# A two-layer spectral and gated-MLP kernel: forward stage in written order with its loads pinned, filter loads without marker copies, row sums from PSUM

## The chip, the cores and the metric

The kernel runs on one core of one Trainium2 chip. The metric is the device time of one execution in microseconds (us). The kernel before took 1263.59 us in the median of three runs (1261.65 to 1268.51). Engines are called by short names: PE is the matmul engine (PEld its weight load), DVE the vector engine, ACT the scalar engine, POOL the GpSimd engine; SP only issues DMAs. SBUF is the on-chip memory, PSUM the eight accumulator banks that PE writes.

## The reference

The input x has 2048 rows of 512 float32 numbers. Two layers follow each other, with the same weights; a layer is a spectral filter and then a bilinear gated MLP, each with a layer norm ahead and a residual sum behind:

```
def _A_ref(x, w_r, w_i):
    X = rfft2(x);  X = X * (w_r + 1j * w_i)
    return irfft2(X, s=(S, D))
def _B_ref(x, w_gate, w_up, w_down):
    return ((x @ w_gate) * (x @ w_up)) @ w_down
x = x + _A_ref(_layernorm(x), A_w_r, A_w_i)
x = x + _B_ref(_layernorm(x), B_w_gate, B_w_up, B_w_down)
...
```

The last two lines are done twice. S is 2048, D is 512, and the MLP is 1792 wide.

## The kernel before, in words

The residual `xs` stays in SBUF as 16 tiles of 128 rows by 512. Each layer goes through these stages:

**Forward stage** (`fwd_steps`, lines 211 to 282). For each tile t: `stats` (bn_stats and bn_aggr on DVE), `rstd` (a square root on ACT and four small DVE instructions), `a0` (loads the twiddle factors `tw`; the half sums and differences `fo`, `fe` of the row on POOL and DVE), `a1` (four transposes `tp` on PE, copied to `fs` by ACT), `a2` (eight instructions of the row transform `dp` on PE, scaled to `us` by ACT), `a3` (eight instructions of the first column transform `sp` on PE into two PSUM banks, copied into `E` by ACT). The work is listed as steps: a tile's `a0`, `a1`, `a2` and `a3` belong to steps b, b+1, b+2 and b+4, and the list is sorted by step. Lines 671 to 683 issue it for the first layer and put between its entries the loads of the spectral filter (`W.load`, 1 MB each, lines 290 to 302) and the splitting of the first two MLP weight blocks (`forms_w`, lines 509 to 533: `rg` is the block as loaded, `wt` its high and low parts; ACT copies the high part, POOL subtracts). A filter load is preceded by a marker, a copy of one element of `E` by POOL into the load's target, so that the load cannot be issued before that tile of `E` is there; `prep_hp` (lines 144 to 151) has a marker too. The twiddle tiles and the small table `wct` share four buffers (tag `tw`).

**Middle phase** (`mid_phase`): the second column transform, the product with the filter, and the way back, over 16 groups of columns. It begins with DVE transposes of `E`, which need all 16 tiles.

**Inverse stage** (`inv_steps`): back to rows (`vp`, `vs`, `yi`), the sum into `xs`, and the next statistics.

**MLP** (`unit`, `beside`, `down_w`): for each of 14 weight blocks seven products (`gx`, `gy`, `gw`, `gz`, `gv`; a Strassen-like scheme, with three float32r matmuls each) and the down product `db`, added to `xs` by DVE. `db` has two PSUM banks (tag `d`), so that the third `db` in a row waits for DVE's sum of the first. Rows are done in two halves. While the first half runs, the rows of the second are normalised (`norm`, which writes `xn`), transposed by PE (`turn`, which writes `tq` into banks of tag `a`, three of them), copied by ACT into `xf` (`stage["t"]`, line 450) and summed (`sums`, lines 471 to 476: four DVE instructions of 128 by 256, all operands in SBUF). `weave` (lines 654 to 665) mixes two lists by the costs that stand in them; the row-sum entry is listed at 0.3.

What sets the order: a scheduler may move instructions on each engine, unless they were issued while `pin["on"]` was set (lines 111 to 130), when they keep the written order among themselves. The MLP runs pinned (line 717). The first forward stage, the end of the second one (lines 766 and 767), the middle phases and the first part of each inverse stage run unpinned. DMA issues on SP are never pinned. Every engine's queue is in order once it is built. All recorded operations carry line 123, that of the helper; the tiles' names tell them apart.

Of the kernel before, what the change touches and what calls it, by code (L numbers as in the profile page):

```python
# [9 lines left out]
F32 = mybir.dt.float32  # L10
F32R = mybir.dt.float32r
AF = mybir.ActivationFunctionType
ALU = mybir.AluOpType
EPS = 1e-5
NF = 14
G0 = [(0,), (1,), (2,), (3,)] + [(t, t + 1) for t in range(4, 16, 2)]
# [71 lines left out]
def kernel(ctx: ExitStack, tc: tile.TileContext, x, wf, wc, wb, dfwd, dinv, tf, ti, mid, out):  # L88
    nc = tc.nc
    PS = bass.MemoryType.PSUM  # L90
    cp = ctx.enter_context(tc.tile_pool(name="cp", bufs=1))
    wk = ctx.enter_context(tc.tile_pool(name="wk", bufs=1))
# [3 lines left out]
    XYW = "xyw"  # L96

    def bank(name, tag):
        return pp.tile([128, 512], F32, name=name, tag=tag, bufs=NB[tag])
# [4 lines left out]
    def f32(ap):  # L104
        return ap.bitcast(F32)
# [2 lines left out]
        for n, (a, b) in enumerate(((sh, mh), (sh, ml), (sl, mh))):  # L108
            TE.matmul(o, a, b, start=start and n == 0, stop=stop and n == 2, skip_group_check=True)

    pin = {"on": False}

    class Queue:


        def __init__(self, engine):
            self.engine = engine

        def __getattr__(self, name):
            f = getattr(self.engine, name)  # L120

            def call(*args, **kw):
                ins = f(*args, **kw)  # L123
                if pin["on"]:
                    tc.keep_in_program_order(ins)
                return ins

            return call

    V, A, G, TE = (Queue(e) for e in (nc.vector, nc.scalar, nc.gpsimd, nc.tensor))  # L130
    tt, stt = V.tensor_tensor, V.scalar_tensor_tensor
    gtt = G.tensor_tensor

# [7 lines left out]
    f2, g2, ident = (midt[:, 128 * i:128 * i + 128] for i in range(3))  # L141
    hp = cp.tile([128, 2, 32, 2], F32, name="hp")

    def prep_hp(after):
        wct = wk.tile([128, 4, 2, 32], F32, name="wct", tag="tw", bufs=4)
        G.tensor_copy(wct[0:1, 0, 0, 0:1], after)
        nc.sync.dma_start(wct, wc)
        for ri, col, src, op, scale in ((0, 0, 0, ALU.add, 0.5), (1, 0, 1, ALU.subtract, 0.5),
                                        (0, 1, 3, ALU.subtract, -0.5), (1, 1, 2, ALU.add, 0.5)):
            tt(hp[:, ri, :, col], wct[:, src, 0], wct[:, src, 1], op)  # L150
            V.tensor_scalar(hp[:, ri, :, col], hp[:, ri, :, col], scale, None, op0=ALU.mult)
# [49 lines left out]

    def twiddle(src, t):
        tw = wk.tile([128, 2, 128], F32, name="tw", tag="tw", bufs=4)
        nc.sync.dma_start(tw, src[:, 2 * t:2 * t + 2])
        return tw

    def in_steps(ops):
# [76 lines left out]
    class Filter:  # L284
# [2 lines left out]
        def __init__(self):  # L287
            self.at = {}

        def load(self, n, after=None):  # L290
            if n < 3:
                if n == 0:
                    self.a = wk.tile([128, 3, 64, 32], F32, name="wq", tag="xA")
                self.at[n] = self.a[:, n]
            elif n < 6:
                t = wk.tile([128, 64, 32], F32, name="wr", tag=("dc", "h", "wd")[n - 3])
                self.at[n] = t
            else:
                self.at[n] = self.a[:, n - 6]
            if after is not None:  # L300
                G.tensor_copy(self.at[n][0:1, 0, 0:1], after)
            nc.sync.dma_start(self.at[n], wf[:, n // 2, n % 2])

        def __call__(self, n, i, lo=0):
            kw = 16 * (n % 4)
# [127 lines left out]
    def build_x(X, nm, tags, stage=None):  # L433

        XA, XS = X
        s = {}
        r = nm["ts"][0] % 4
        cols = slice(128 * r, 128 * r + 128)

        def norm():  # L440
            s["xn"] = [normed(t, nm) for t in nm["ts"]]

        def turn(h):
            tq = bank("tq", tags[h])
            xn = s["xn"][h]
            for i in range(4):
                TE.transpose(tq[:, 128 * i:128 * i + 128], xn[:, 128 * i:128 * i + 128], ident)
            s[h] = tq.rearrange("p (b k s) -> p b k s", b=2, k=2)
            if stage is not None:
                A.copy(stage["t"][:, r, 2 - 2 * h:4 - 2 * h], s[h])  # L450

        def forms():
            a, b = s[0], s[1]
            S = wk.tile([128, 4, 2, 128], F32, name="sx", tag=("sx", "rg")[r % 2])
            A.copy(S[:, 1:4:2], a)
            A.copy(S[:, 2], b[:, 0])
            A.copy(S[:, 0], b[:, 1])
            A.copy(XA[:, 1:3, 0, :, cols], a)
            A.copy(XA[:, 0, 0, :, cols], b[:, 1])
            gtt(S[:, 0], S[:, 2], S[:, 0], ALU.add)  # L460
            gtt(S[:, 2], S[:, 1], S[:, 2], ALU.subtract)
            gtt(S[:, 1], S[:, 0], S[:, 1], ALU.subtract)
            gtt(S[:, 3], S[:, 3], S[:, 1], ALU.subtract)
            tt(XA[:, 1:3, 1, :, cols], a, f32(XA[:, 1:3, 0, :, cols]), ALU.subtract)
            tt(XA[:, 0, 1, :, cols], b[:, 1], f32(XA[:, 0, 0, :, cols]), ALU.subtract)
            A.copy(XS[:, :, 0, :, cols], S)
            for h in (0, 2):
                gtt(XS[:, h:h + 2, 1, :, cols], S[:, h:h + 2], f32(XS[:, h:h + 2, 0, :, cols]), ALU.subtract)
            s.clear()

        def sums():
            G_ = stage["t"][:, r]
            tt(G_[:, 4], G_[:, 0], G_[:, 1], ALU.add)
            tt(G_[:, 6], G_[:, 2], G_[:, 0], ALU.subtract)
            tt(G_[:, 5], G_[:, 4], G_[:, 2], ALU.subtract)
            tt(G_[:, 7], G_[:, 3], G_[:, 5], ALU.subtract)

        def high():
            A.copy(XA[:, :, 0, :, cols], stage["t"][:, r, 1:4])
            A.copy(XS[:, :, 0, :, cols], stage["t"][:, r, 4:8])  # L480

        def low_a():
            tt(XA[:, :, 1, :, cols], stage["t"][:, r, 1:4], f32(XA[:, :, 0, :, cols]), ALU.subtract)

        def low_s(h):
            gtt(XS[:, h:h + 2, 1, :, cols], stage["t"][:, r, 4 + h:6 + h], f32(XS[:, h:h + 2, 0, :, cols]), ALU.subtract)

        if stage is not None:
            return ([(0.2, norm), (0.43, lambda: turn(0)), (0.43, lambda: turn(1)), (0.3, sums)],
                    [(0.5, high), (0.5, lambda: low_s(0)), (0.5, low_a), (0.5, lambda: low_s(2))])  # L490
        return [(0, norm), (0.43, lambda: turn(0)), (0.43, lambda: turn(1)), (0, forms)]

    raws, ws, wds, hs_ = {}, {}, {}, {"n": 0}
# [7 lines left out]
    def load_raw(first=False):  # L501
        if first:
            todo.pop(0)
        if todo and todo[0] is not None:
            ft = todo.pop(0)
            raws[ft] = wk.tile([128, 4, 256], F32, name="rg", tag="rg")
            nc.sync.dma_start(raws[ft], wb[ft, :, 0:8].rearrange("p (b k) f -> p b (k f)", k=2))

    def forms_w(ft):

# [156 lines left out]
    dcs = {}  # L667
    dcs["f"] = load_df()
    E = wk.tile([128, 16, 257, 2], F32, name="E", tag="e")
    W = Filter()  # L670
    load_raw()
    pre = []
    for ft in range(2):
        f = {**forms_w(ft), "next": load_raw}
        pre += [[f[k] for k in g.split()] for g in ("start h0", "h12 l0", "d0", "l12", "d1", "d2", "d3 h34", "h56 l34", "l56 next")]
    for n, o in enumerate(fwd_steps(lambda: dcs["f"], E, lambda t: ("d", "a", XYW[2 * t % 3], XYW[(2 * t + 1) % 3]), G0, lambda t: False)):
        o[-1]()
        if n >= 40 and n % 2 and pre:
            for f in pre.pop(0):
                f()  # L680
        if n in (30, 38, 46, 54, 62):
            W.load((0, 1, 2, 4, 5)[(n - 30) // 8], E[0:1, n // 8 - 3, 0, 0:1])
    prep_hp(E[0:1, 10, 0, 0:1])

    for layer in range(2):
        W.load(3)
        mid_phase(E, W)
        X = (wk.tile([128, 3, 2, 2, 512], F32R, name="xA", tag="xA"),
# [35 lines left out]
        stage = {}  # L724
        both = [build_x(X, nms[ts[0]], ("a", "a"), stage) for ts in pairs[4:]]
        inv2.append((0, lambda: stage.update(t=wk.tile([128, 4, 8, 2, 128], F32, name="xf", tag="e"))))
        pre = [p for p, _ in both]
# [10 lines left out]
        if layer == 0:  # L738
            dcs["f"] = load_df()
            E = wk.tile([128, 16, 257, 2], F32, name="E", tag="e")  # L740
# [12 lines left out]
        if layer == 0:  # L753
            early = lambda t: "aaaa"
            late = lambda t: ("d", "a", XYW[2 * t % 3], XYW[(2 * t + 1) % 3])
            K = 7
            fb = fwd_steps(lambda: dcs["f"], E, early, [(8, 9), (12, 13)], lambda t: False)
            fc = [(o[0] + K, *o[1:]) for o in fwd_steps(lambda: dcs["f"], E, late, [(10, 11), (14, 15)], lambda t: False)]
            weave(ops, [o for o in fb if o[0] < K])
            W = Filter()  # L760
            for m in range(3):
                W.load(m)
            emit(last)
            W.load(4)
            W.load(5)
            pin["on"] = False
            emit(in_steps([o for o in fb if o[0] >= K] + fc))
        else:
            put = lambda t: nc.sync.dma_start(out[:, t], xs[:, t])
            weave(ops, [(0, 0, 0.1, lambda t=t: put(t)) for t in (8, 9, 12, 13)])  # L770
            for k, o in enumerate(last):
                o[-1]()
                put((10, 11, 14, 15)[k])
# [40 lines left out]
```

## Time and profile before

| | us |
|---|---|
| median of three runs | 1263.59 |
| lowest, highest | 1261.65, 1268.51 |
| the profiled execution | 1267.91 |
| its span, first to last instruction | 1266.1 |

The profile is of one execution. Its page gives the busy time of each engine, the span cut in 40 slices of 31.65 us with the granted PE clock in tenths, the chain of waits that ended last, and groups of like instructions. The trace behind it answers for any stretch of time: a timeline (start, length, engine, instruction, and in brackets the idle time ahead of it and what ended it), waits, and tables by stretch. Of the whole span PE is busy 92%, DVE 71%, POOL 57% and ACT 34%. In this execution the first forward stage goes from 0 to 76.3 us, the first layer's middle phase starts there, the row sums of the first layer lie from 353 to 384 us and of the second from 976 to 1005 us, and the second forward stage ends at 701.2 us.

### The profile page before, as it was taken

The page shows a single profiled execution, that of the slowest core. Times are in us where ns is not written, and L with a number is a line of the kernel's source. Part 1 is how long each engine was busy: PE and PEld are TensorE (multiplying, and loading weights), DVE is VectorE, ACT ScalarE, POOL GpSimd, SP SyncE. Part 2 cuts the span into 40 slices and gives each one's busy share as a digit, 9 for nine tenths or more (in the row PEclk, how much of TensorE's full clock was granted, in tenths as well). Part 3 has the DMA queues.
Part 4 walks back from the last instruction along what each step waited for, and adds up shares of the span by engine and source line. Part 5 has one row for each costly group of instructions (what it writes and reads, how often), then busy time and mean ns, then how long its engine had stood idle before and what let it go on. Part 6 is the DMA issues. An engine that isn't in the chain of part 4 may idle for free.

```text
span 1266.1 us, 16697 instructions
## 1 busy us (share of the span) xinstructions
PE 1165.0 (92%) x5932; PEld 950.3 (75%) x5932; DVE 894.7 (71%) x1681; ACT 428.1 (34%) x863; POOL 727.6 (57%) x756
## 2 busy tenths in 40 slices
PE   5989679999988999999989886999999799999998
PEld 4745668888777877888777465888887689788887
DVE  8458656677777787775676786567678777666676
ACT  3566233222322232333314643332233232322221
POOL 4434348666645486775651434676675545877772
PEclk9899899999988999999999998999999799999999
DMA  6432011111120011112104310021111110211111
GB/s 225 184 122 74 18 34 50 59 51 49 57 67 18 1 42 54 44 53 67 42 1 188 146 42 25 18 72 52 36 50 50 58 59 34 67 59 50 34 35 67
DMA packets 30755, 77.69 MB, mean 61 GB/s; under 512 B 3408, under 2 KB 11856, under 8 KB 28368
## 3 DMA queue, kind: packets, MB, share of 16 engines
q1 hardware_dynamic: 29952, 73.54, 17.5%
q0 software_dynamic: 288, 2.10, 0.5%
q8 instruction: 47, 0.77, 0.2%
q10 hardware_dynamic: 432, 0.98, 0.2%
q14 instruction: 36, 0.29, 0.1%
HBM read 72.42 MB, written 4.19 MB: 61 GB/s over the span
## 4 chain that ended last, share of the span: by engine, by line
PE 56%; POOL 18%; DVE 12%; issue 8%; ACT 4%; DMA 1%; POOLq 0%; SPq 0%; DVEq 0%; ACTq 0%
PE db L123 16%; PE gz L123 8%; PE gx L123 7%; POOL wt L123 6%; POOL rg L123 4%; PE gw L123 4%; PE gv L123 4%; PE gy L123 4%; DVE xs L123 3%; PE yi L123 3%; PE dp L123 3%; DVE q L123 2%; PE sp L123 2%; POOL jz L123 2%; PE vp L123 2%
## 5 line engine op out<-in xcount | busy, mean ns | idle before, releaser
L123 PE MATMUL db<-wd,h 128*128 128x512 f32 x1344 | 372.0, 403 | 26.3 <-DVE xs L123 22.5
L123 DVE TENSOR_TENSOR xs<-xs,db 128x512 f32<-128x512 f32 x448 | 296.6, 681 | 49.7 <-PE db L123 49.6
L123 POOL TENSOR_TENSOR h<-q,h 128x512 fp32r<-128x512 f32 (+1 forms) x144 | 152.6, 1063 | 278.4 <-ACT h L123 186.4
L123 PEld LDWEIGHTS db<-wd,h 128*128 128x128 f32 x1344 | 247.1, 193 | 80.6 <-DVE xs L123 31.2
L123 POOL TENSOR_TENSOR wt<-rg,wt 128x512 fp32r<-128x512 f32 (+1 forms) x216 | 235.2, 1095 | 92.7 <-ACT wt L123 92.0
L123 ACT CAST h<-q 128x512 fp32r<-128x512 f32 (+1 forms) x144 | 75.6, 526 | 344.7 <-DVE q L123 325.5
L123 PE MATMUL gx<-xA,wt 128*128 128x512 f32 (+1 forms) x864 | 184.2, 350 | 2.7 <-ACT s L123 2.7
L123 ACT CAST wt<-rg 128x512 fp32r<-128x512 f32 (+1 forms) x216 | 110.5, 540 | 186.7 <-POOL rg L123 173.4
L123 PEld LDWEIGHTS gx<-xA,wt 128*128 128x128 f32 x864 | 143.3, 194 | 24.6 <-ACT s L123 4.4
L123 POOL TENSOR_TENSOR rg<-rg 128x256 f32<-128x256 f32 x200 | 149.6, 748 | 11.0
L123 DVE TENSOR_TENSOR q<-gy,s 128x512 f32<-128x512 f32 (+1 forms) x72 | 41.1, 571 | 149.9 <-ACT wt L123 78.5
L123 PE MATMUL gw<-xS,wt 128*128 128x512 f32 (+1 forms) x432 | 93.8, 351 | 17.3 <-ACT xS L123 9.7
L123 PEld LDWEIGHTS gw<-xS,wt 128*128 128x128 f32 x432 | 71.6, 194 | 30.4 <-ACT xS L123 10.6
L123 PE MATMUL gz<-xS,wt 128*128 128x512 f32 (+1 forms) x432 | 92.9, 352 | 0.0
L123 PE MATMUL gy<-xS,wt 128*128 128x512 f32 (+1 forms) x432 | 92.2, 351 | 0.0
L123 PE MATMUL gv<-xS,wt 128*128 128x512 f32 (+1 forms) x432 | 89.5, 343 | 0.0
L123 PE MATMUL gz<-xA,wt 128*128 128x512 f32 (+1 forms) x432 | 89.0, 341 | 0.0
L123 PEld LDWEIGHTS gz<-xS,wt 128*128 128x128 f32 x432 | 74.8, 196 | 13.7 <-issue 0.7
L123 PEld LDWEIGHTS gz<-xA,wt 128*128 128x128 f32 x432 | 72.1, 188 | 12.0
L123 PEld LDWEIGHTS gv<-xS,wt 128*128 128x128 f32 x432 | 71.8, 188 | 12.3 <-issue 0.3
L123 PEld LDWEIGHTS gy<-xS,wt 128*128 128x128 f32 x432 | 72.2, 197 | 9.3
L123 POOL TENSOR_TENSOR wd<-rw,wd 128x512 fp32r<-128x512 f32 x52 | 68.3, 1314 | 6.4 <-ACT wd L123 6.4
(92 smaller groups left out, 1547.8 us busy)
## 6 DMA issues: line engine op xcount, KB each, us to landing
rg<-in_wb_dram SPq DMA_DIRECT2D x50, 512.0 KB, 3.6
rw<-in_wb_dram SPq DMA_DIRECT2D x52, 256.0 KB, 2.7
wq<-in_wf_dram SPq DMA_DIRECT2D x10, 1024.0 KB, 5.8
wr<-in_wf_dram SPq DMA_DIRECT2D x6, 1024.0 KB, 6.0
tw<-in_tf_dram SPq DMA_DIRECT2D x32, 128.0 KB, 2.1
tw<-in_ti_dram SPq DMA_DIRECT2D x32, 128.0 KB, 2.1
out_dram<-xs SPq DMA_DIRECT2D x16, 256.0 KB, 2.0
xs<-in_x_dram SPq DMA_DIRECT2D x7, 512.0 KB, 7.8
```

The costliest lines, as they stand in the source:

```text
L123: ins = f(*args, **kw)
```

## The change

- `pin` gets a second flag, `loads`, and SP an order-keeping wrapper that goes by it. The loads of twiddles, filter, `wct` and MLP gate and up blocks are issued through it. In the first forward stage both flags are set; they are cleared at the start of each layer. The line that cleared the pin ahead of the end of the second forward stage is gone, so that this end is pinned too (its loads are not).
- Filter loads and `prep_hp` have no markers. `wct` is loaded at step 3 and used at step 6. The first `rg` load is issued at step 5 and no longer ahead of the stage; three pieces of weight splitting go in front of each step from 5 on; filter loads go in front of steps 6, 8, 10, 12 and 14.
- The row sums of the second half take `tq` in PSUM as one operand. They are split in two entries of 0.2 each, in place of one of 0.3, which also shifts the other entries of the weave.

```diff
-    pin = {"on": False}
+    pin = {"on": False, "loads": False}
...
-                if pin["on"]:
+                if pin[self.flag]:
                     tc.keep_in_program_order(ins)
...
+    SP = Queue(nc.sync, "loads")
...
-        G.tensor_copy(wct[0:1, 0, 0, 0:1], after)
-        nc.sync.dma_start(wct, wc)
...
-            if after is not None:
-                G.tensor_copy(self.at[n][0:1, 0, 0:1], after)
-            nc.sync.dma_start(self.at[n], wf[:, n // 2, n % 2])
+            SP.dma_start(self.at[n], wf[:, n // 2, n % 2])
...
         def sums():
             G_ = stage["t"][:, r]
-            tt(G_[:, 4], G_[:, 0], G_[:, 1], ALU.add)
-            tt(G_[:, 6], G_[:, 2], G_[:, 0], ALU.subtract)
-            tt(G_[:, 5], G_[:, 4], G_[:, 2], ALU.subtract)
-            tt(G_[:, 7], G_[:, 3], G_[:, 5], ALU.subtract)
+            tt(G_[:, 4], s[1][:, 1], G_[:, 0], ALU.add)
+            tt(G_[:, 6], s[0][:, 0], G_[:, 0], ALU.subtract)
+
+        def sums2():
+            G_ = stage["t"][:, r]
+            tt(G_[:, 5], G_[:, 4], s[0][:, 0], ALU.subtract)
+            tt(G_[:, 7], s[0][:, 1], G_[:, 5], ALU.subtract)
...
-            return ([(0.2, norm), (0.43, lambda: turn(0)), (0.43, lambda: turn(1)), (0.3, sums)],
+            return ([(0.2, norm), (0.43, lambda: turn(0)), (0.43, lambda: turn(1)), (0.2, sums), (0.2, sums2)],
...
-    load_raw()
-    pre = []
+    pre = [load_raw]
     for ft in range(2):
         f = {**forms_w(ft), "next": load_raw}
-        pre += [[f[k] for k in g.split()] for g in ("start h0", "h12 l0", "d0", "l12", "d1", "d2", "d3 h34", "h56 l34", "l56 next")]
-    for n, o in enumerate(fwd_steps(...)):
+        pre += [f[k] for k in "start h0 h12 l0 d0 l12 d1 d2 d3 h34 h56 l34 l56 next".split()]
+    pin.update(on=True, loads=True)
+    step = 0
+    for o in fwd_steps(...):
+        if o[0] > step:
+            step = o[0]
+            if step == 3:
+                load_hp()
+            if step == 6:
+                prep_hp()
+            if step in (6, 8, 10, 12, 14):
+                W.load((0, 1, 2, 4, 5)[step // 2 - 3])
+            if step > 4:
+                for f in pre[:3]:
+                    f()
+                del pre[:3]
         o[-1]()
-        if n >= 40 and n % 2 and pre:
-            for f in pre.pop(0):
-                f()
-        if n in (30, 38, 46, 54, 62):
-            W.load((0, 1, 2, 4, 5)[(n - 30) // 8], E[0:1, n // 8 - 3, 0, 0:1])
-    prep_hp(E[0:1, 10, 0, 0:1])
...
     for layer in range(2):
+        pin.update(on=False, loads=False)
...
-            pin["on"] = False
             emit(in_steps([o for o in fb if o[0] >= K] + fc))
```

More of the change, by code (lines that the diff above doesn't have):

```diff
@@ L109, in mm3, with __init__ @@
             TE.matmul(o, a, b, start=start and n == 0, stop=stop and n == 2, skip_group_check=True)
-    pin = {"on": False}
+    pin = {"on": False, "loads": False}
     class Queue:
-        def __init__(self, engine):
-            self.engine = engine
+        def __init__(self, engine, flag="on"):
+            self.engine, self.flag = engine, flag
         def __getattr__(self, name):
@@ L142, with load_hp, prep_hp @@
     hp = cp.tile([128, 2, 32, 2], F32, name="hp")
-    def prep_hp(after):
-        wct = wk.tile([128, 4, 2, 32], F32, name="wct", tag="tw", bufs=4)
-        G.tensor_copy(wct[0:1, 0, 0, 0:1], after)
-        nc.sync.dma_start(wct, wc)
+    wcs = {}
+    def load_hp():
+        wcs["t"] = wk.tile([128, 4, 2, 32], F32, name="wct", tag="tw", bufs=4)
+        SP.dma_start(wcs["t"], wc)
+    def prep_hp():
+        wct = wcs["t"]
         for ri, col, src, op, scale in ((0, 0, 0, ALU.add, 0.5), (1, 0, 1, ALU.subtract, 0.5),
@@ L203, in twiddle @@
         tw = wk.tile([128, 2, 128], F32, name="tw", tag="tw", bufs=4)
-        nc.sync.dma_start(tw, src[:, 2 * t:2 * t + 2])
+        SP.dma_start(tw, src[:, 2 * t:2 * t + 2])
         return tw
@@ L288, in __init__, with load @@
             self.at = {}
-        def load(self, n, after=None):
+        def load(self, n):
             if n < 3:
@@ L506, in load_raw @@
             raws[ft] = wk.tile([128, 4, 256], F32, name="rg", tag="rg")
-            nc.sync.dma_start(raws[ft], wb[ft, :, 0:8].rearrange("p (b k) f -> p b (k f)", k=2))
+            SP.dma_start(raws[ft], wb[ft, :, 0:8].rearrange("p (b k) f -> p b (k f)", k=2))
     def forms_w(ft):
@@ L670 @@
     W = Filter()
-    load_raw()
-    pre = []
+    pre = [load_raw]
     for ft in range(2):
         f = {**forms_w(ft), "next": load_raw}
-        pre += [[f[k] for k in g.split()] for g in ("start h0", "h12 l0", "d0", "l12", "d1", "d2", "d3 h34", "h56 l34", "l56 next")]
-    for n, o in enumerate(fwd_steps(lambda: dcs["f"], E, lambda t: ("d", "a", XYW[2 * t % 3], XYW[(2 * t + 1) % 3]), G0, lambda t: False)):
-        o[-1]()
-        if n >= 40 and n % 2 and pre:
-            for f in pre.pop(0):
-                f()
-        if n in (30, 38, 46, 54, 62):
-            W.load((0, 1, 2, 4, 5)[(n - 30) // 8], E[0:1, n // 8 - 3, 0, 0:1])
-    prep_hp(E[0:1, 10, 0, 0:1])
+        pre += [f[k] for k in "start h0 h12 l0 d0 l12 d1 d2 d3 h34 h56 l34 l56 next".split()]
+    pin.update(on=True, loads=True)
+    step = 0
+    for o in fwd_steps(lambda: dcs["f"], E, lambda t: ("d", "a", XYW[2 * t % 3], XYW[(2 * t + 1) % 3]), G0, lambda t: False):
+        if o[0] > step:
[10 more added lines that the diff above has]
+                del pre[:3]
+        o[-1]()
+    assert not pre
     for layer in range(2):
+        pin.update(on=False, loads=False)
         W.load(3)
```

## The prediction

> **What bounds the kernel now.** I read the page first, then the table by stretches, then waits and timeline where PE stood idle. On the page PE is the fullest engine:
>
> ```profile
> span 1266.1 us, 16697 instructions
> ...
> PE 1165.0 (92%) x5932; PEld 950.3 (75%) x5932; DVE 894.7 (71%) x1681; ACT 428.1 (34%) x863; POOL 727.6 (57%) x756
> ...
> PEclk9899899999988999999999998999999799999999
> ```
>
> So time is won where PE waits or its granted clock is low. The table by stretches (length, busy time of the engines, granted clock, DMA) shows where in the first forward stage that is:
>
> ```profile
> 20.00:36.00 16.00, 12.38 (x51) 8.16 (x50) 13.62 (x42) 7.05 (x19) 11.14 (x16) 0.69 0.51 189
> 36.00:48.00 12.00, 12.00 (x84) 9.77 (x82) 4.41 (x11) 8.10 (x17) 2.31 (x4) 0.99 0.76 285
> 48.00:60.00 12.00, 10.07 (x47) 7.08 (x44) 6.27 (x7) 5.29 (x13) 9.39 (x11) 0.72 0.14 46
> ```
>
> From 36 to 48 us PE is full: the chain there repeats dp 1.31, sp 1.07, tp 0.59, so a tile costs 2.97 and sixteen cost 47.5 us; the stage takes 76.3. The rest goes in stretches like 48 to 60. The timeline:
>
> ```profile
> 50.16 0.77 POOL L123 TENSOR_TENSOR rg<-rg 128x256 f32<-128x256 f32 x1
> ...
> 50.96 0.62 ACT L123 CAST wt<-rg 128x512 fp32r<-128x512 f32 x1 [2.68 <-POOL rg L123]
> ...
> 51.91 1.13 PE L123 MATMUL sp<-us,tw 64*128 64x257 f32 x6 [1.15 <-ACT E L123]
> ```
>
> An ACT cast of the weight split waits 2.68 for POOL, the copy to `E` behind it is late, and PE waits 1.15 for its bank. The chain that ended last shows what follows (start, length): eight `dp` take 2.93, not 1.31; the clock has fallen.
>
> ```profile
> 54.62 2.93 PE dp L123 x8
> ```
>
> The other place is the row sums, here in the first layer (timeline, then the waits of PE from 340 to 400 us: total, times, longest):
>
> ```profile
> 365.14 2.93 PE L123 MATMUL db<-wd,h 128*128 128x512 f32 x6 [4.84 <-DVE xs L123]
> ...
> 385.16 2.93 PE L123 MATMUL db<-wd,h 128*128 128x512 f32 x6 [3.83 <-DVE xs L123]
> ```
> ```profile
> PE db L123 <- DVE xs L123: 9.5, 4, 4.8
> ```
>
> DVE is busy with `xf` and `xn`, so its sums that free the `db` banks come late. Durations by shape (min/median/max, ns) tell why `xf` is slow:
>
> ```profile
> L123 DVE TENSOR_TENSOR xf<-xf x32: 415/721/1515, 353.1 to 1004.7; 128x256 f32<-128x256 f32 x32
> ```
> ```profile
> L123 DVE TENSOR_TENSOR xs<-xs,db x448: 653/680/691, 169.2 to 1262.2; 128x512 f32<-128x512 f32 x150
> ```
>
> `xf` has both operands in SBUF and spreads from 415 to 1515, most where POOL works; `xs<-xs,db` has one in PSUM and in 448 runs never leaves 653 to 691. The second layer has the same waits (9.5 in all, from 960 to 1020).
>
> **The forward stage, part by part.** I follow the built order of each engine by hand with these rows. DVE has `fe` of tiles 0 to 3 at about 6.8, 9.3, 11.3 and 13.3 (about 2 us a tile, from 0.6 stats, 0.4 `fo`, 0.5 `fe` and 0.4 to 0.5 small ones). PE starts at the low clock (the first eight `dp` took 2.77), so dp1 ends near 14.8. sp0 needs the first twiddle, which stands behind 4.8 MB that move at some 410 GB/s: about 14.1 plus its own time, so sp0 ends at about 16.1.
>
> A wait is added here. `wct` now takes the third of the four `tw` buffers, so the twiddle of tile 3 waits on SP until sp0 is done (before, the fifth twiddle left SP at 22.2, as the first `sp` ended), and the first `rg` load is queued behind it: issued at about 16.8, landing 3.6 later (page, median) at 20.4. ACT has the cast of that `rg` ahead of the copy of tile 0 to `E`, so behind the cast wait `E`, `fs` and `us`, and PE waits in sp1 from 18.2 to 21.3, **3.1 us**. POOL's split then runs 0.73 for 256 columns and 1.26 for 512 between its `fo`, and ends near 31; the clock costs some 2.4 (a slow `dp` and `sp` against fast ones). The second `rg` needs the same single buffer, lands near 35, and ACT again has its casts ahead of an `E` copy: sp5 waits **1.2** and ends at 37.3. What is left on PE is 8 tp, 9 dp, 10 sp = 4.7 + 11.8 + 10.7 = 27.2: 64.5, and 0.8 for the last `E` copy. That is 65.3, or 67.8 if the second wait costs the clock too; I take 66.3, **10.0 won**. Bounds: with no wait at all PE would fill from 12.9 and the stage end at 58.2 (18 won); with both `rg` landing in the 6.7 of the first 130 us and the clock lost twice, 73 (3 won).
>
> The POOL markers go: six copies of 0.17 to 0.37, 1.1 us; they cost nothing before, since POOL stood idle 19.8 ahead of its `fo`, and cost nothing now. Filter loads then lie in the queue beside twiddles; 8 MB (five filter MB, two `rg`, the twiddles) in 60 us are a third of what 410 GB/s carry. DVE's 6.6 wait for `wct` goes, but it ended at 71.2 and the transposes wait for `E` until 76.3: worth 0. The filter's fourth MB still waits for `df` to be free; it was issued at 73.2 and needed at 89.1, so it stays hidden.
>
> The pinned end of the second forward stage: PE's order differs in one `sp` instruction, DVE does four `db` sums ahead of the statistics. PE waited 0.5 for `fe` at 689; DVE's list now gives each `fe` 0.5 to 1 before PE needs it. I take 0, bounds -1.5 and +1.5.
>
> **The row sums.** Sixteen `xf` instructions per layer take 11.8 us (mean 779). With a PSUM operand the nearest row is `q<-gv` of 128x256, 425; back to back, 0.37. Four then take 1.5, not 4.13 (at 357.8) or 3.77 (at 379.9). The banks of `tq` are held until the second pair of sums; there are three, and by my times the tightest reuse has 2 us to spare. What matters is PE. Now, per layer, it loses 4.84 + 3.83 in waits, 1.1 in smaller ones near 341 to 346, and to the clock: 2.93 + 2.76 against 1.36 each (about 2.9) and db 2.93, gz 1.28, db 2.30 against 1.39, 0.71, 1.39 (3.0): **15.7**. In the new order two things change. At 340 to 345 two `db` stand together where a `tq` and a `gz` stood between, and DVE has two `xn` (2.0) between the sums that free their banks: PE waits 1.35 + 1.85. At the former 365, xn 2.2, four xf 1.5, xn 2.2, q 1.4 and one xs end 1.45 after PE is ready; at the former 385, 1.4 after. New waits 6.05, and I let the first cost the clock (2.7): 8.75. **Won: 7.0 per layer, 14.0 in all.** Bounds: 9.6 per layer with no loss of clock, 1.2 if it is lost each time (8.4). The rest of the weave moves `vp` and `yi` by one entry between 186 and 340 us, where the trace has no PE wait: 0.
>
> **Sum.** 10 + 14 = 24. From the profiled 1267.9 (span 1266.1 and 1.8 around it): 1243.9. The median lies 4.3 lower, so 1239.6; I predict **1240**.
>
> **A rule against a row.** At 51.9 and 54.6 PE waited only 1.15 and 0.78, and the clock fell at once. The Trainium skill, "TensorE: Matmul & The Clock Gate", Part 1, has the clock halved only after an idle window of about 3.4 us. This row speaks against that; by the rule none of my new waits would cost clock.
>
> **Rivals.**
> - *The clock holds in the short waits.* Mechanism: waits up to 3 us lie between full stretches. For it: 1.37 in the middle phase (91.4) was followed by matmuls at full speed. Against it: 54.6. Won 12.4 + 19.2 = 31.6: **1232**.
> - *The row sums give nothing*, as PE's waits move from the sums to the pairs of `db` and `xn`. For it: the new wait at 340. Won 10 to 12: **1253**.
> - *The forward stage gives nothing*: pinning does not do what it says, because the cast order and the DMA fill set the pace as before. Against it: 36 to 48 us ran full in the same order. Won 14: **1250**.
> - *Slower.* ACT in written order behind the weight casts. If each split stops ACT from the load's issue to POOL's last difference (6.7 + 4.9 = 11.6, twice) and each stop costs 3 of clock twice over, the stage takes 58.2 + 23.2 + 12 = 93.4, 17 more than before; with the row sums at 2.4 that is 15 slower: **1278**. It decides once PE's waits in the stage pass 18 us. Against it: ACT is busy 8.1 of 12 us in the full stretch, so it can catch up.
>
> **Chances.** Forecast 0.45, clock holds 0.20, no gain from sums 0.15, none from the stage 0.12, slower 0.08. A measurement of this kernel tells about 0.5%, 6.3 us, from no change: below 1257.3 is faster. Of the two middle rivals about a third ends above that: faster 0.82, same 0.11, slower 0.07. The range leaves out the slower case and the tails: 1228 (nearly all bounds at their best, 36 won) to 1256.
>
> **What would show it.** The first DVE transpose of `E` at 66 and not 76; an ACT cast of `rg` waiting for a DMA near 17 to 20, with PE waiting for `E` behind it; full 2.97 steps from 37 on. In the sums `xf` at 410 to 430 ns whatever POOL does; no PE wait above 2 us near the former 365 and 385, and a new one of 1 to 2 at the former 343. I am wrong if PE's clock falls as often as before, if a step is set by ACT, or if `tq` waits for a bank.

## The result, and the profile after

The changed kernel takes 1250.55 us in the median of four runs (1249.99 to 1254.64). Beside them the kernel before took 1266.05 (four runs, 1261.65 to 1269.65): a ratio of 0.9886, 95% interval 0.9844 to 0.9929. Later, beside other kernels, it ran again: 1246.16 in five runs, ratio 0.9846 (0.9824 to 0.9869). So it is faster by 1.1 to 1.5%, by more than the 0.5% that can be told from no change. The profiled execution took 1250.0 us, 17.9 less than that of before. The page (span; busy time and share; the granted clock in 40 slices):

```profile
span 1248.2 us, 16685 instructions
...
PE 1155.3 (93%) x5932; PEld 940.9 (75%) x5932; DVE 887.4 (71%) x1681; ACT 424.6 (34%) x863; POOL 725.2 (58%) x750
...
PEclk8999899999999999999999998999999999999999
```

PE's busy time went from 1165.0 to 1155.3 with the same 5932 matmuls: some 10 of the 18 us are a clock that is granted more often, the rest are waits. Of the slices, the two 8s at 348 to 411 us and the 7 at 981 to 1013 us, where the row sums lie, are now 9s.

Where the time went is read from events that both traces have, and from what lies between them:

| event (us) | before | after | the stretch before it got shorter by |
|---|---|---|---|
| first transpose of `E` on DVE (end of the first forward stage) | 76.3 | 72.9 | 3.4 |
| issue of `di` by POOL (middle phase) | 98.6 | 95.2 | 0.0 |
| first `xS` on POOL (row sums, first layer) | 405.5 | 395.1 | 6.9 |
| first four `fo` of the second forward stage | 659.2 | 647.7 | 1.1 |
| first transpose of `E`, second layer | 701.2 | 688.7 | 1.0 |
| issue of `di`, second layer | 722.0 | 709.5 | 0.0 |
| first `xS`, second layer | 1027.1 | 1009.1 | 5.5 |
| end | 1266.1 | 1248.2 | -0.1 |

The row sums gave 12.4 of the forecast 14.0. The first forward stage gave 3.4 of the forecast 10.0. The row sums first: durations by shape (min/median/max, ns), then the waits of PE from 320 to 400 us (total, times, longest):

```profile
L123 DVE TENSOR_TENSOR xf<-tq,xf x24: 414/421/426, 348.5 to 989.5; 128x256 f32<-128x256 f32 x24
L123 DVE TENSOR_TENSOR xf<-xf,tq x8: 410/413/415, 349.7 to 989.1; 128x256 f32<-128x256 f32 x8
```
```profile
PE db L123 <- DVE xs L123: 4.4, 3, 1.9
```

No `xf` leaves 410 to 426 any more, and the waits are less than half of the former 9.5. Where they lie now (timeline of PE; in brackets the wait and who ended it):

```profile
341.58 0.97 PE L123 MATMUL db<-wd,h 128*128 128x512 f32 x3 [1.88 <-DVE xs L123]
343.50 1.65 PE L123 MATMUL db<-wd,h 128*128 128x512 f32 x3 [0.96 <-DVE xs L123]
345.66 2.17 PE L123 MATMUL gz<-xS,wt 128*128 128x512 f32 x6
...
377.55 1.66 PE L123 MATMUL db<-wd,h 128*128 128x512 f32 x6 [1.59 <-DVE xs L123]
```

The new wait at the former 343 came, in two pieces, and cost the clock: three `db` take 1.65 right behind it, as long as six take at 377.55. Behind the later 1.59 the clock stays.

In the forward stage, the table by stretches (length, busy time and count of PE, PEld, DVE, ACT, POOL, then granted clock, DMA share, GB/s):

```profile
20.00:36.00 16.00, 12.99 (x66) 9.74 (x66) 12.39 (x26) 8.59 (x21) 11.42 (x13) 0.79 0.56 189
36.00:48.00 12.00, 11.30 (x73) 9.02 (x72) 11.05 (x27) 8.47 (x22) 7.38 (x9) 1.00 0.76 262
48.00:60.00 12.00, 9.94 (x56) 7.44 (x55) 10.95 (x28) 5.91 (x15) 5.17 (x7) 0.86 0.30 107
```

DVE's column, the third pair, is what I had not counted on: from 36 to 60 us it is busy 22 of 24 us, where it was 10.7 before. The timeline of PE shows both losses:

```profile
23.01 2.07 PE L123 MATMUL sp<-us,tw 64*128 64x257 f32 x6 [3.08 <-ACT E L123]
25.01 2.93 PE L123 MATMUL dp<-df,fs 128*128 128x256 f32 x8
...
39.31 1.13 PE L123 MATMUL sp<-us,tw 64*128 64x257 f32 x6 [0.70 <-ACT E L123]
...
51.38 0.33 PE L123 MATMUL tp<-midt,fe 128*128 128x128 f32 x1 [1.66 <-DVE fe L123]
52.11 0.33 PE L123 MATMUL tp<-midt,fe 128*128 128x128 f32 x1 [0.40 <-DVE fe L123]
52.28 1.80 PE L123 MATMUL dp<-df,fs 128*128 128x256 f32 x8
54.01 2.18 PE L123 MATMUL sp<-us,tw 64*128 64x257 f32 x8
```

The wait of 3.08 for the copy of `E`, behind the cast of the first `rg`, and the small one at 39 are the forecast ones. The wait for `fe` at 51 is not, nor the slow `sp` of 2.18 behind it. DVE just before, from its timeline:

```profile
46.07 0.69 DVE L123 BATCH_NORM_STATS2 st<-xs 128x6 f32<-128x512 f32 x1
...
47.26 1.85 DVE L123 SCALAR_TENSOR_TENSOR rs<-rs 128x2 f32<-128x2 f32 x2
49.03 1.56 DVE L123 SCALAR_TENSOR_TENSOR fo<-xs,rs 128x256 f32<-128x256 f32 x1
50.70 1.36 DVE L123 TENSOR_TENSOR fe<-fo 128x128 f32<-128x128 f32 x2
```

Two instructions over two columns take 1.85 us together (each of this kind takes 0.16 in the median), one `fo` 1.56 (median 0.485), two `fe` 1.36 (median 0.29 each). In the same time POOL runs the subtractions of the weight split, 1.27 each. The statistics `st` read one operand and keep their 0.69.

### The profile page after: what moved, and what is told of

Its sections match the earlier page's. It is cut to its first block, busy times and chain, and to the rows that moved or that the text cites. A ratio compares the mean times of both kernels' runs of the same rounds, so it can differ in the third digit from the quotient of the medians.

```text
span 1248.2 us, 16685 instructions
## 1 busy us (share of the span) xinstructions
PE 1155.3 (93%) x5932; PEld 940.9 (75%) x5932; DVE 887.4 (71%) x1681; ACT 424.6 (34%) x863; POOL 725.2 (58%) x750
## 4 chain that ended last, share of the span: by engine, by line
PE 54%; POOL 18%; DVE 13%; issue 8%; ACT 5%; DMA 2%; POOLq 0%; DVEq 0%; ACTq 0%; SPq 0%
PE db L123 15%; PE gz L123 8%; PE gx L123 7%; POOL wt L123 6%; PE gw L123 4%; POOL rg L123 4%; DVE xs L123 4%; PE gv L123 4%; DVE q L123 4%; PE dp L123 3%; PE yi L123 3%; PE gy L123 3%; PE sp L123 3%; POOL jz L123 2%; PE vp L123 2%
## 5 line engine op out<-in xcount | busy, mean ns | idle before, releaser
L123 PE MATMUL db<-wd,h 128*128 128x512 f32 x1344 | 365.1, 398 | 17.1 <-DVE xs L123 12.0
L123 PEld LDWEIGHTS db<-wd,h 128*128 128x128 f32 x1344 | 241.4, 189 | 73.0 <-DVE xs L123 25.1
L123 DVE TENSOR_TENSOR q<-gy,s 128x512 f32<-128x512 f32 (+1 forms) x72 | 41.1, 571 | 147.1 <-ACT wt L123 82.2
L123 PE MATMUL gw<-xS,wt 128*128 128x512 f32 (+1 forms) x432 | 93.4, 350 | 19.5 <-ACT xS L123 11.8
L123 PEld LDWEIGHTS gz<-xS,wt 128*128 128x128 f32 x432 | 72.9, 191 | 13.1 <-issue 0.7
L123 PEld LDWEIGHTS gv<-xS,wt 128*128 128x128 f32 x432 | 71.9, 188 | 12.3 <-issue 0.3
```

## Experiments

The theory after the result: the row sums are faster because one operand is in PSUM; the forward stage gains little because DVE, now in written order with its statistics in line, is slowed by POOL's weight split, and because of the wait for `rg`. Two measures serve throughout. T is the first transpose of `E`. R is the time from the issue of `di` to the first `xS`, given for the first and second layer. The ratio is to the kernel before, run on the same chip.

**The sums alone** (the kernel before with this edit only):

```diff
-            tt(G_[:, 4], G_[:, 0], G_[:, 1], ALU.add)
+            tt(G_[:, 4], s[1][:, 1], G_[:, 0], ALU.add)
...
+        def sums2():
...
-            return ([..., (0.3, sums)],
+            return ([..., (0.2, sums), (0.2, sums2)],
```

> The kernel before with the row sums alone changed (operands in PSUM, two entries of the weave); forward stage, markers and tail as before. Theory (the sums won about 12.4 of the 17.9 us between the two profiled spans): span near 1253.5, ratio near 0.990, first POOL xS at 405.5 - 7 = 398.5, xf at 410 to 430 ns, PE waits for xs between 325 and 405 us 4.4 instead of 9.5. Rival (the two changes help each other: without the shorter stage the sums give only what the row durations give, 16 x 0.35 = 5.6 us a layer off DVE and half of it on PE): 5 to 6 us in all, ratio 0.995.

1252.41, ratio 0.9889 (0.986 to 0.9918): 14.1 us of 1267.2. T 76.0, R 300.3 and 299.5 against 306.9 and 305.1 before; waits of 4.9. The theory's numbers, within 4 us of span.

**The stage alone** (the kernel after with the sums and the end of the second forward stage as before):

```diff
-            tt(G_[:, 4], s[1][:, 1], G_[:, 0], ALU.add)
+            tt(G_[:, 4], G_[:, 0], G_[:, 1], ALU.add)
...
-            return ([..., (0.2, sums), (0.2, sums2)],
+            return ([..., (0.3, sums)],
...
+            pin["on"] = False
             emit(in_steps([o for o in fb if o[0] >= K] + fc))
```

> The kernel after with the old row sums and the old unpinned end of the second forward stage: only the first forward stage is new (written order, pinned loads, no markers). Theory: the first transpose of E at 72.9 as in after, and everything behind it shifted by the same 3.4: span near 1262.7, ratio 0.997. Rival (the stage itself was worth the forecast 10 and something else in after costs 6): first transpose near 66, span near 1256, ratio 0.992.

1263.11 (ten runs), ratio 0.996 (0.9943 to 0.9977): 5.1 us. T 71.4, R 305.3 and 307.0. So the two parts add up: 14.1 and 5.1 make 19.2, and the whole change measured, by the ratios of its two sets in the same way, 14.4 and 19.5 (15.5 and 21.4 by the medians). The rival, a stage worth 10, is out: the interval ends at 7.2.

**The first `rg` load ahead of the stage:**

```diff
-    pre = [load_raw]
+    load_raw()
+    pre = []
```

> The kernel after, with the first rg load issued ahead of the stage instead of at step 5, behind the twiddle of tile 3. Theory (two separate losses: the load, and DVE slowed by POOL's weight split from 42 to 52 us): the PE wait of 3.1 at 23 us goes, the slow steps at 42 to 52 and the lost clock behind them stay or come earlier; first transpose of E at 69 to 71 instead of 72.9, ratio to before about 0.986. Rival (one loss: the clock falls at the first stall and everything later follows from it): no slow step at 42 to 52, first transpose at 64 or below, ratio 0.981.

1244.29, ratio 0.9821 (0.9804 to 0.9839). T 69.4: the long wait for `E` is gone (one of 0.9 is left), the waits for `fe` are the same 5.0 in all. The range for T held, but what I read from it did not. T of the unchanged stage turned out to vary (below), from 68.2 to 72.9, and 69.4 lies in the middle. The ratio is below the theory's 0.986, and its interval lies just under that of the change's first runs (from 0.9844), but overlaps that of the later ones (from 0.9824). No gain from the early load can be shown from this; in the trace PE arrives earlier at its next wait for DVE or POOL. The rival falls too, for no run here reached 64 with the split in its place.

**The weight split behind the stage:**

```diff
-            if step > 4:
-                for f in pre[:3]:
-                    f()
-                del pre[:3]
         o[-1]()
-    assert not pre
+    for f in pre:
+        f()
```

> The kernel after, with the whole weight split of the first two weight tiles, and its two rg loads, issued behind the forward stage. Theory (DVE in written order is slowed by POOL's split and ACT by the load): with neither in the stage DVE's small operations stay under 0.4 us, no PE wait above 1.5 us after 15 us, first transpose of E at 59 to 62; the split then lies in the middle phase, where POOL has its jz products, and costs some of the 11 to 14 us back: total between 1242 and 1256. Rival (DVE in written order is itself too slow, 2.5 us or more a tile with its statistics in line, whatever POOL does): first transpose at 68 to 73, DVE busy over 90% from 36 to 60 us.

1245.34, ratio 0.9826 (0.981 to 0.9843). T **60.5**, in the range of the theory. The same stretches in its table:

```profile
20.00:36.00 16.00, 15.81 (x106) 12.45 (x106) 14.38 (x45) 9.37 (x24) 4.28 (x6) 1.00 0.71 264
36.00:48.00 12.00, 12.00 (x82) 9.58 (x82) 10.78 (x33) 8.65 (x22) 3.20 (x5) 1.00 0.43 154
48.00:60.00 12.00, 12.00 (x79) 9.05 (x77) 1.57 (x8) 7.14 (x16) 0.00 (x0) 1.00 0.41 129
```

With POOL at its `fo` alone, DVE does the same work in the same written order and starts its last `fe` at 49.3, not 61.2; PE is full and its clock whole from 20 us on. This is the "27.2 of full PE" of the prediction, and it needs POOL out of DVE's way. The edit takes ACT's casts and both loads out of the stage too; that it is POOL that slows DVE rests on the durations: in the stage after the change, nine `fo` on DVE had no POOL instruction beside them and took 483 to 485 ns, the seven others up to 1562. The gain does not last: the split now fills POOL in the middle phase, which takes 30.4 us and not 20.8 to 22.3, with one wait of 3.6 for `ys`. Of the 8 to 12 us won (60.5 against 68.2 to 72.9), 8 to 10 were given back.

**The sums in two entries, but from SBUF:**

```diff
-            tt(G_[:, 4], s[1][:, 1], G_[:, 0], ALU.add)
-            tt(G_[:, 6], s[0][:, 0], G_[:, 0], ALU.subtract)
+            tt(G_[:, 4], G_[:, 0], G_[:, 1], ALU.add)
+            tt(G_[:, 6], G_[:, 2], G_[:, 0], ALU.subtract)
...
```

> The kernel after, with the two entries of row sums in their new places but all operands in SBUF again (the copies of the rows that ACT makes), as before. Theory (the operand in PSUM is what counts: xf at 415 to 430 ns instead of 415 to 1515): xf is back at a median near 700 and a maximum near 1500, PE waits for xs from 320 to 400 us of 7 or more instead of 4.4, from the issue of di to the first POOL xS 304 to 307 us as in before (306.9) and not 300.0 as in after; ratio about 0.994. Rival (the new order of the weave, sums split in two entries, does it): waits 4.4 to 5, 300 us, ratio 0.988.

1268.19 (ten runs), ratio 1.0009 (0.999 to 1.0029): nothing at all is left, although the stage kept its gain (T 68.2). R 310.4 and 308.7, longer than before. Durations of `xf`, PE's waits in the first layer's sums, and one of them:

```profile
L123 DVE TENSOR_TENSOR xf<-xf x32: 410/723/1511, 342.1 to 1004.1; 128x256 f32<-128x256 f32 x32
```
```profile
PE db L123 <- DVE xs L123: 11.0, 6, 3.8
```
```profile
379.53 2.93 PE L123 MATMUL db<-wd,h 128*128 128x512 f32 x6 [3.82 <-DVE xs L123]
```

The operand in PSUM is what counts, and by this one profile the new order is worse than the old. The theory had the sign right and the size too small (ratio 0.994).

**The sums from PSUM, but in one entry:**

```diff
-        def sums2():
-            G_ = stage["t"][:, r]
...
-            return ([..., (0.2, sums), (0.2, sums2)],
+            return ([..., (0.3, sums)],
```

> The kernel after, with the four row sums in one entry of the weave as in before, but with their operands in PSUM. Theory (the operand in PSUM is what counts): 299.5 to 301.5 us from the issue of di to the first POOL xS, PE waits for xs of 4 to 6 us, ratio as of after, 0.987 to 0.990. Rival (the split in two entries counts): one long stretch of DVE again, PE waits of 7 or more, ratio 0.993 or above.

1243.28, ratio 0.9806 (0.9776 to 0.9837): better than the change. R 296.2 and 297.5, below the range that I gave; waits of 4.0. With these the four cases make a square (means of R over both layers and all profiled kernels of the kind; in brackets how many values):

| R, us | one entry | two entries |
|---|---|---|
| operands in SBUF | 306.1 (4 values) | 309.6 (2) |
| one operand in PSUM | 296.4 (6) | 299.8 (16) |

The operand is worth 9.7 a layer in either order, the second entry costs some 3.5 with either operand; single values in a cell lie up to 4.5 apart, and one cell rests on a single profile. The trace shows what the 3.5 are: with one entry the pair of waits at 341 is not there (0.19 and 0.64 are left), and nothing slow follows. The remaining waits of this kernel, 1.54 and 1.59, do not touch the clock:

```profile
352.67 1.65 PE L123 MATMUL db<-wd,h 128*128 128x512 f32 x6 [1.54 <-DVE xs L123]
367.94 1.65 PE L123 MATMUL db<-wd,h 128*128 128x512 f32 x6 [1.59 <-DVE xs L123]
```

**The weight split from step 11 on**, with the early load:

```diff
-            if step > 4:
+            if step > 10:
                 for f in pre[:3]:
...
```

> The kernel after, with the first rg load ahead of the stage and the weight split started at step 11 of the forward stage and not at 5; the order of everything else is kept. Theory (DVE in written order runs ahead of PE by some 10 us where POOL leaves it alone, and POOL's split slows it by 10 us in all): with the lead built up first, DVE ends its last fe at 52 to 55 us, the first transpose of E comes at 61 to 64 (60.5 with no split in the stage, 69.4 with the split from step 5), and the middle phase does not pay for the split as it did with the split behind the stage: span 1233 to 1236, ratio 0.975 to 0.979. Rival (what the split costs is the same wherever it lies beside DVE's forward work): first transpose at 67 or later, ratio 0.982.

1243.6, ratio 0.9806 (0.977 to 0.9843). T 63.4 and the last `fe` at 51.8, as the theory has it: DVE builds its lead first, POOL's split comes when little of DVE's work is left, and the middle phase keeps its 20.8. But the total does not show the 6 us: the profiled span is 1242.3. The end of the second forward stage and the parts of the second layer, which this edit does not touch, took 7 us longer than in the run with the early load. One profile cannot tell whether that belongs to the edit, so the next three kernels ran side by side in five rounds.

**Split from step 11 and sums in one entry; the same with the split from step 5; the change as it is:**

> The kernel after, with the first rg load ahead of the stage, the weight split from step 11 on, and the four row sums (operands in PSUM) in one entry of the weave. Theory (each part is worth what its own stretch showed: 5 to 9 in the stage, 3 a layer from the single entry): first transpose of E at 62 to 65, 296 to 298 us from di to the first POOL xS in both layers, total 1229 to 1237, ratio to before 0.970 to 0.976 and 0.987 or less to the copy of after beside it. Rival (what is won early is lost later to the clock, as the split from step 11 alone seemed to show): 1240 or more, ratio 0.980.

> The same with the weight split from step 5. Theory: only the stage differs from the kernel with the split from step 11, first transpose at 68 to 71 for 62 to 65, all else as there: 4 to 7 us slower, 1235 to 1242. Rival (the place of the split is worth nothing in the total): the same total within 2 us.

> The kernel after once more, beside the other two, for its own spread. Theory (the stage takes 68.2 to 72.9 with one and the same order, as the clock falls at the first stall or not; the first profile of after drew the worst): first transpose anywhere from 68 to 73, median 1245 to 1252, ratio 0.984 to 0.989. Rival (72.9 is its fixed value): 72 to 74, ratio 0.9886 or above.

| | median | ratio, interval | T | R |
|---|---|---|---|---|
| split from 11, one entry | 1235.43 | 0.9758 (0.9735 to 0.9782) | 65.0 | 298.0, 295.2 |
| split from 5, one entry | 1240.32 | 0.9783 (0.9763 to 0.9803) | 70.0 | 294.9, 296.5 |
| the change | 1246.16 | 0.9846 (0.9824 to 0.9869) | 68.2 | 299.6, 299.9 |

The first is the fastest kernel of this study, 32 us under before and 10.7 under the change. The place of the split shows 4.9 us in the total, as in T, though the intervals of these two overlap a little; the 7 us above were not the edit's. The early load and the single entry together make 5.8. Against the change I had expected 0.987 or less and got 0.991 by the medians, since the change itself did better than in its first runs.

The third row settles T: the same stage in the same order took 72.9, 71.4, 68.2, 68.5 and 68.2 in five profiled kernels, 69.8 in the mean. From 48 to 60 us the granted clock was 1.00 in the three at 68 and 0.86 in the two others, with the same instructions. But the clock is not the first link. Ahead of its fall PE waited 1.66 and 1.65 for `fe` in the two slower kernels, and 0.87 to 0.88 in the other three, because DVE met POOL at another point: the two `rs` that took 1.85 at 47.26 above took 0.36 in the copy of the change (DVE, then PE):

```profile
44.68 0.36 DVE L123 SCALAR_TENSOR_TENSOR rs<-rs 128x2 f32<-128x2 f32 x2
```
```profile
48.59 0.33 PE L123 MATMUL tp<-midt,fe 128*128 128x128 f32 x1 [0.87 <-DVE fe L123]
```

DVE starts its last two `fe` at 61.2 in the slowest and at 58.0 in the fastest of the five, so 3.2 of the 4.7 us between them are there before PE's last tiles. What set off the other meeting is not shown; the first stall was longer too, 3.08 and 2.45 against 2.26 to 2.34. At that first stall the clock fell in four of the five, and not in the kernel with the sums in one entry:

```profile
21.61 1.13 PE L123 MATMUL sp<-us,tw 64*128 64x257 f32 x6 [2.34 <-ACT E L123]
22.67 1.57 PE L123 MATMUL dp<-df,fs 128*128 128x256 f32 x8
```

Here eight `dp` take 1.57 behind the stall, where 25.01 above has 2.93. Even with the clock held, T is 68 and DVE busy 11.2 of 12 us from 36 to 48: the slowed DVE, not the clock, is most of what is missing to 60.5. Up to T, DVE's same 139 instructions keep it busy for 48.3 us in the kernel with the sums in one entry, and for 41.1 with the split behind the stage, at a granted clock of 1.00 in both (third pair; POOL is the fifth):

```profile
0.00:68.50 68.50, 54.03 (x320) 40.94 (x320) 48.34 (x139) 35.66 (x83) 27.13 (x36) 1.00 0.59 209
```
```profile
0.00:60.50 60.50, 51.67 (x320) 40.38 (x320) 41.09 (x139) 33.13 (x76) 12.02 (x20) 1.00 0.63 229
```

So the profile of the result drew the worst of five; the stage is worth 6.3 in the mean (76.1 less 69.8).

**Nothing pinned in the stage, and only the engines pinned:**

```diff
-    pin.update(on=True, loads=True)
+    pin.update(on=False, loads=False)
```

(in the second kernel `on=True, loads=False`).

> The kernel after with nothing pinned in the first forward stage: the scheduler orders engines and loads, the markers stay gone, loads and split are issued at the new steps. Theory (the written order on the engines is what the stage won): the scheduler draws statistics forward as in before and PE starts late again, first transpose of E at 74 to 78, ratio 0.988 to 0.992. Rival (the markers and the place of the loads did it): 68 to 73 and the ratio of after, 0.985 to 0.988.

> The kernel after with the four compute engines pinned and the loads on SP not. Theory (SP's order matters little, since 8 MB in 60 us leave the queue idle most of the time and the first rg load stays behind the twiddle of tile 2 or 3 either way): first transpose of E at 68 to 73 as with all pinned, PE waits for E of 2.3 to 3.1 near 21 to 23 us, ratio 0.984 to 0.989. Rival (pinning the loads was needed): first transpose at 74 or later.

Nothing pinned: 1251.74, ratio 0.9884 (0.9848 to 0.9919), T 74.3. Engines pinned: 1245.84, ratio 0.9843 (0.9801 to 0.9886), T 67.0. By T, markers and new steps give 1.8 and the written order on the engines the other 4 to 5, each from one profile; 1.8 is less than the 4.7 by which T varies, so it is not shown. The totals, run side by side, show the written order: 1250.52 to 1252.43 with nothing pinned, 1245.11 to 1247.95 with the engines pinned. Pinning the loads shows no gain. With loads free the first `rg` stands ahead of the twiddle of tile 3 on SP, and the wait for `E` is 0.4, not the 2.3 to 3.1 that I gave: the pinned loads made that wait. Yet T is only 1.2 under the lowest of the five above, 1 under the 68 that I gave, with that wait gone and the clock at 1.00 from 20 us on. This agrees with the early load: the wait was not what set T.

## Why the prediction was right, and where it was not

Forecast 1240 in 1228 to 1256, faster; measured 1250.55, and 1246.16 in the later set. The sign holds and the result lies in the range, but not near its middle; **one term of the two was mis-sized**. Of the 10.5 us by which 1240 misses 1250.55, 2.5 are the starting point: it was the median of three runs, 1263.6, and with the fourth run it is 1266.05 (1266.7 to 1268.4 in later sets).

- *Row sums, 14.0 by the likeliest value: right.* 12.4 between the profiles, 14.1 as a part by itself (10.4 to 17.7). `xf` at 410 to 430 came out; the waits at the former 365 and 385, forecast as 1.45 and 1.4, shrank to a single one of 1.59; the new one at 341, forecast as 1.35 and 1.85, came as 1.88 and 0.96 and cost the clock, as assumed for the first wait alone. That this new wait was a loss of the second entry, 3.5 a layer, and not a price of the operand, the prediction did not see.
- *First forward stage, 10.0: wrong by a third to two thirds* (3.4 in the profile, 6.3 in the mean of five, 5.1 as a part by itself). The start held: the load was issued at 17.8 (forecast 16.8), the cast ran at 22.3 (20.4), PE waited 3.08 (3.1), then 0.70 (1.2), with the end of that `sp` at 40.4 (37.3): 3 late by the load and the clock. In the three kernels with T at 68 that end came at 37.6 to 37.9. What failed is the step "what is left on PE is ... 27.2", with full steps of 2.97 from 37 on: with the last copy of `E` it forecast 28.0 from there to T, and 32.5 passed in the profile, 30.6 in each of those three. It rested on DVE needing about 2 us a tile. That figure was taken at 6 to 13 us, where POOL has little to do, and it was too small even there: after the change `fe` of tiles 1 to 3 came at 9.8, 12.3 and 15.0, 2.5 to 2.7 apart. That alone would still fit under 2.97. With the weight split beside it, DVE needs 3.1 a tile (22 us busy for seven tiles from 36 to 60 us), more than PE's 2.97, and becomes the bound. The split behind the stage, with all else in place, gave T 60.5: from the same `sp` to T it was 28.3 there, so 27 to 28 us of PE is right when DVE is free. I had used just this slowing of operations with both operands in SBUF for `xf`, and not applied it to `fo`, `fe` and `rs` in the stage, which have both in SBUF too.
- *Why the old stage showed no such bound:* its scheduler drew the statistics forward into the time when PE waited; in the stretch that I took as the model (36 to 48 us, DVE busy 4.4 of 12) DVE had only `fo` and `fe` left. In written order each tile carries its own statistics, and the stretch was no model for it.
- *Markers 0, `wct` 0, middle phase 0: no run speaks against it.* The 1.8 of T from markers and new steps together lies inside the spread of T and is not split further. *The pinned end of the second forward stage, 0:* right. From the first four `fo` to the transposes 41.9 in the mean of eleven profiled kernels with it, 41.8 of three without.
- *The 1.1 us between the row sums and the second forward stage* are probably not the change's: 253.6 in the profile of before, and 252.4 and 252.6 in the two kernels that hold one part of the change each.
- *The low clock at the start* was read from 2.77 for the first eight `dp`. The granted clock in the tables is 1.00 up to 20 us, in before too, so no row shows what slowed them.
- *Rivals.* By the number alone 1250.55 stands nearer to two rivals than to the forecast: 1250 (the stage gives nothing) and 1253 (the sums give nothing). Neither mechanism was at work, since the stage by itself gave 5.1 (2.9 to 7.2) and the sums 14.1. "The clock holds in the short waits" was half true: it holds behind single waits of 1.5 to 1.6 and once behind 2.34, but T with a held clock is 68, not 58, so its 1232 needed a stage that the order does not give. "The sums give nothing" was near for the wrong reason: it does hold with operands in SBUF (ratio 1.0009). "Slower, by ACT" did not begin: PE waited 14.1 in the whole stage, 3.8 of it for ACT, against the 18 from which it decides.

On the clock, the rows are: behind 1.88 and 0.96 with 0.97 of work between them it fell (three `db` 1.65); behind 1.66 and 0.40 it fell (`sp` 2.18); behind 3.08 and 2.45 it fell at once; behind 2.26 and 2.31 it fell in two kernels one group of `sp` later, and behind 2.34 in a third not at all; behind 1.54 and 1.59 it held; behind a single 1.07, for a copy of `E` in the fastest kernel (51.67), it fell within 2 us (eight `dp` 2.77). No length of a wait divides these rows. The Trainium skill, "TensorE: Matmul & The Clock Gate", Part 1, has the clock follow PE's activity in a free-running window of about 3.4 us. A free-running window agrees with waits of 2.26 to 2.45 at one place that are followed by a fall at once, by one a group late, or by none. That a whole idle window is needed does not: here two waits that make 2.06 in all were enough, and one of 1.07.

The slowing itself is the other rule that can be weighed. In the square above, the one step of putting an operand in PSUM took the spread of `xf` from 410 to 1511 down to 410 to 426 ns. The Trainium skill, "SBUF — State Buffer", section "SBUF: two separate sides", says that a DVE operation with two SBUF inputs and a POOL operation that reads SBUF exclude each other for the length of an instruction. The trace agrees. In the profile of before, the 12 `xf` of 32 that had no POOL instruction beside them took 415 to 426 ns, and the other 20 took 418 to 1515; after the change 25 of 32 had POOL beside them, and none took more than 426. It holds down to operations over two columns: the `rs<-rs` of the stage took up to 163 ns without POOL and up to 1199 with it.

What stays open: what sets the clock's choice behind one and the same stall, and where the change as it stands loses the difference between its two sets of runs (1250.55 and 1246.16, on other chips or at other times). A part can be seen: the profiled execution of the later set took 1250.15 with T at 68.2, and lost nearly 4 us behind the first layer's sums, where one `db` waited 3.34 for DVE at 462 and the clock fell; in the profile of the first set the wait at this place was 1.4.

## What to carry to other kernels

A duration from one stretch is no price for another: ask which engine works beside it there, above all POOL beside DVE operations with both inputs in SBUF. When a scheduler's order is replaced by a written one, add up every engine's work per step anew, not only that of the fullest one; an engine at half load in the old order may have had its work done earlier. Put an operand where it needs no shared access, and let the second engine's bulk work start when the first has built its lead: here they were worth 9.7 us a layer and 4.9 us in all, while the load's wait of 3, taken away by itself, showed no sure gain.

## What the runs showed of the hardware that was not expected

- A DVE operation of 128 by 2 with both inputs in SBUF takes 0.16 us in the median and up to 1.20 while POOL subtracts; a `fo` of 128 by 256 takes 0.485 and up to 1.56. The excess, 1.04 and 1.08, is alike for both and lies within the length of one POOL instruction (0.73 to 1.28), so tiny operations suffer most for their size. One tensor operand is no full protection: `rs<-mv` (TENSOR_SCALAR, 128 by 2) took 0.166 in the median and up to 0.563. By shape in the stage, after:

```profile
L123 DVE SCALAR_TENSOR_TENSOR rs<-rs x20: 159/162/1199, 8.3 to 60.6; 128x2 f32<-128x2 f32 x12, 128x1 f32<-128x1 f32 x8
L123 DVE SCALAR_TENSOR_TENSOR fo<-xs,rs x16: 483/485/1562, 5.6 to 60.6; 128x256 f32<-128x256 f32 x16
```

- One stage in one order differs by up to 4.7 us between kernels that share it, with the clock and with where DVE meets POOL. The middle phase takes 20.8 us at a granted clock of 1.00 or 22.3 at 0.92: behind the same wait of 1.22 for `T` the first four `zp` take 1.98 or 3.68. Gains of this size are not to be read from one profile: 3.4 and 8.1 would both have been "the" result.
